# Low parts of three of a pair's five plain activation blocks made by GpSimd instead of VectorE, block means turned with two value tiles

## The chip, the cores and the metric

The kernel runs on one core of one Trainium2 chip. The metric is the device time of one launch in microseconds (us), less is better. Five engines with a queue each work side by side: TensorE (PE in the rows; its weight loads are PEld), VectorE (DVE), ScalarE (ACT), GpSimd (POOL), and SyncE (SP), which here only issues DMA transfers. Each queue is worked off in order; an instruction that has to wait holds up all that stand behind it on its engine.

## What is computed

The reference is a local attention with block summaries, followed by two feed-forward layers:

```
k_sum = k.reshape(B, H, nb, block, D).max(axis=3)
v_sum = v.reshape(B, H, nb, block, D).mean(axis=3)
scores_l = where(|i - j| < 16, scale * q k^T, -1e9)
scores_s = scale * q k_sum^T + log(block)
a = softmax(concat(scores_l, scores_s))
x = a @ concat(v, v_sum)                      # 2 batches, 8 heads, 768 tokens, 64 wide
xn = x / rms(x) * rms_g                       # 1536 tokens x 512
y  = (silu(xn @ w_gate) * (xn @ w_val)) @ w_out      # 512 -> 1536 -> 512
out = (s * relu(y @ w_in)**2 + b) @ w_out2           # 512 -> 2048 -> 512
```

A block is 32 tokens, so there are 24 block sums per head. The weights come in double precision.

## The kernel before

**Number format.** Every operand of a dense product is split into a high part (the value rounded to the format that TensorE takes at full pace) and a low part (value minus high part), and a product is three matmuls: high x high, low x high, high x low. For weights, ScalarE scales a loaded 128x512 unit (line 243), VectorE puts bits together in three instructions (lines 253 to 255), ScalarE makes the high part (line 268) and GpSimd the low part (line 272). One such unit is wanted every few microseconds for nearly the whole run, and a helper that is called at fixed places of the code (`slot`, `w_ahead`, `feed`) writes these steps between the others.

**Attention.** It runs in the first 110 us: 12 tiles of 128 tokens. A planner (`give_out`, line 472) sets the order: it holds a list of tasks, each with engine, assumed duration, rank and what it depends on, plays them on five assumed clocks, and writes the instructions of a task when its turn comes. The order inside each engine's queue is thus fixed when the program is built. Where the planner finds TensorE with nothing to do, it writes a filler matmul (line 557). For the first batch the value rows are turned on TensorE from a tile with the head dimension on partitions (`turn_v`, line 400): 12 windows of 96 rows, each put to its place by ScalarE or VectorE (`put_w`, lines 407 and 409). Under the 96 rows of each window stand 24 rows of block means. The first NMEAN windows get them from an additional set of four turning matmuls (line 398, which reads the 24 block sums that VectorE makes, line 387, as well), the others by a DMA that copies the 24 rows from windows 0 and 1 (`spread_v`; line 172 issues every transfer). The product of weights and values (line 740) of a tile waits for its windows and their means.

**First feed-forward layer.** Gate and value products (`gate`, `val`, `mm12`: lines 903, 904, 909) of a hidden unit are three groups of 12 matmuls, one for each 512 tokens. Between them stand "pairs" (`pair`, lines 1266 to 1268), in which two hidden units of 128 meet w_out in a scheme of seven products in place of eight for the first 1024 tokens; the last 512 tokens are done plainly. A pair needs nine activation blocks, each 128x512 with high and low part: five plain ones (b11, b21, b22, z0, z1: an activation as it is) and four combinations (t1 to t4, made by GpSimd at line 1116). `blocks` writes these out and `split` makes the two parts: the high part on ScalarE (line 1080 or 1082), the low part at line 1083 on the engine that it is given. Pairs 2, 4 and 6 go through `blocks` (pair 0 has its own function, and pair 2 has the b11 and z0 of its first unit ready from elsewhere, so that only z1, b21 and b22 of its plain blocks are split here).

**PSUM.** In this stage the products take turns on seven banks; an eighth is scratch for the weight bits. A bank comes free when VectorE has read it: line 1053 (gate: needs ScalarE's tanh of line 1052 first), line 1065 (value) or line 1274 (pair). When all seven are full, TensorE waits.

**Order of the stage.** gate 6, val 6, pair 2, gate 7, val 7, pair 4, gate 8, gate 9, pair 6, val 8, val 9. The blocks of pair 2 are made during gate and val 6, those of pair 4 during gate and val 7, those of pair 6 during gates 8 and 9. Low parts and combinations stand on the queues of VectorE and GpSimd between the weight work of the same time.

Of the kernel before, what the change touches and what calls it, by code (L numbers as in the profile page):

```python
# [38 lines left out]
PAIRS = (0, 2, 4, 6)  # L39
OUT = 4  # L40
TURN = (0,)
NMEAN = 4
LAT = 0.09
AHEAD = 4.0
IDLE = 0.6
# [13 lines left out]
def kernel(ctx: ExitStack, tc: tile.TileContext, q_t, k_t, v_w, v_t, w_gate, w_val, w_out, w_in2, w_out2, vecs, out):  # L59
    nc = tc.nc  # L60
# [31 lines left out]
    def r(ap):  # L92
        return ap.bitcast(F32R)
# [90 lines left out]
    def after(d, fn):  # L184
        later[d].append(fn)
# [15 lines left out]
    for kind, m in order:  # L201
# [6 lines left out]
        elif kind in ("gates", "vals"):  # L208
            n, ws = len(units), w_gate if kind == "gates" else w_val
            units += [ws[m], ws[m + 1], n, n + 1]  # L210
        elif kind == "pair":
            n = len(units)
            units += [w_out[m], w_out[m + 1], n, n + 1]
        elif kind == "two":
            n = len(units)
# [169 lines left out]
    def sum_vt(b, j):  # L385
        c0 = j * 128 + KW
        nc.vector.tensor_reduce(out=vs[:, c0:c0 + NS], in_=vt0[:, j * KL + WIN:j * KL + WIN + SEQ].rearrange("p (n i) -> p n i", i=BLK), axis=AX.X, op=ALU.add)

    def mean_vt(b, i):
        ps = mean_ps[b] = bank(i)  # L390
        for j in range(NPAIR):
            nc.tensor.transpose(ps[:, j * 128:(j + 1) * 128], vs[:, j * 128:(j + 1) * 128], ident)

    def turn_v(b, w, i, mean):
        ps = mean_ps[b, w] = bank(i)
        for j in range(NPAIR):
            if mean:
                nc.tensor.transpose(ps[0:KC, j * 128:(j + 1) * 128], vs[:, j * 128:j * 128 + KC], ident)
            k0 = j * KL + HQ * w
            nc.tensor.transpose(ps[0:KW, j * 128:(j + 1) * 128], vt0[:, k0:k0 + KW], ident)  # L400

    def put_w(b, w, eng, mean):
        rows = KC if mean else KW
        o = vslot(b, w)[0:rows, :, 0:HD]
        a = mean_ps[b, w][0:rows].rearrange("p (h d) -> p h d", d=HD)
        if eng == "DVE":
            nc.vector.tensor_scalar(out=o, in0=a, scalar1=share[0:rows], scalar2=None, op0=ALU.mult)
        else:
            nc.scalar.activation(out=o, in_=a, func=AF.Copy, scale=share[0:rows])

    def put_v(b, s, eng):
        o = vslot(b, s)[KW:KC, :, 0:HD]
        a = mean_ps[b][KW:KC].rearrange("p (h d) -> p h d", d=HD)
        if eng == "DVE":
            nc.vector.tensor_scalar(out=o, in0=a, scalar1=1.0 / BLK, scalar2=None, op0=ALU.mult)
        else:
            nc.scalar.activation(out=o, in_=a, func=AF.Copy, scale=1.0 / BLK)

    def spread_v(b, s0, n):
        a = vst[b][0][KW:KC, 0:2].rearrange("p (o e) h d -> p o (e h d)", o=1).broadcast_to([NS, n // 2, 2 * NH * VH])  # L420
        o = vst[b][s0 // NTL][KW:KC, s0 % NTL:s0 % NTL + n]
        fetch(out=o.rearrange("p (o e) h d -> p o (e h d)", e=2), in_=a)
# [40 lines left out]
    def task(eng, us, fn, deps=(), rank=0.0, take=(), give=(), bank=None, free=(), more=0.09):  # L463

        t = dict(eng=eng, us=us, fn=fn, deps=[d for d in deps if d is not None], rank=rank, take=take, give=give,
                 bank=bank, free=free, more=more, end=None)
        tasks.append(t)
        return t
# [91 lines left out]
    def dve(n):  # L560
        return 0.07 + 1.042e-3 * n

    def act(n):
        return 0.13 + 0.74e-3 * n

    def pl(n):
        return 0.1 + 2.42e-3 * n
# [4 lines left out]
    def plan(x):  # L572
# [15 lines left out]
        def lvt(b, j, rank):  # L588
            VL[b, j] = task("SP", mb(128 * KL * 4), lambda: load_vt(b, j), [SV[0, j], *(WT[0, w] for w in range(2 * NTL))] if b else (), rank=rank)
# [23 lines left out]
        def means(b, rank):  # L613
            if b == 0:
                zero.append(task("POOL", pl(512) / 3, lambda: nc.gpsimd.memset(vs, 0.0), rank=-28))
            sums = [task("DVE", dve(768), lambda j=j: sum_vt(b, j), [VL[b, j], *zero, *([VM[0]] if b else ())], rank + 0.1 * j) for j in range(NPAIR)]
            for j in range(NPAIR):
                SV[b, j] = sums[j]
            if b in TURN:
                puts = {}  # L620
                for w in range(2 * NTL):
                    m = w < NMEAN
                    rw = (rank + 1.5 + 0.4 * w) if w < 4 else w - 4.0 + 12 * b
                    T = WT[b, w] = task("PE", 0.88 if m else 0.44, lambda i, w=w, m=m: turn_v(b, w, i, m),
                                        [*([*sums] if m else [VL[b, j] for j in range(NPAIR)]), *([VM[0]] if b else ()), ci], rw, bank="M")
                    e = "ACT" if w % 4 != 1 else "DVE"
                    puts[w] = task(e, act(512) if e == "ACT" else dve(512), lambda w=w, e=e, m=m: put_w(b, w, e, m), [T, O[b, w // 2]], rw, free=(T,))
                    VM[b, w // 2, "ok"] = [puts[k] for k in range(w // 2 * 2, w + 1)]
                    if b == 1 or w == 2 * NTL - 1:
                        VM[b] = T  # L630
                if NMEAN < 2 * NTL:
                    for t, n in ((2, 2), (3, 6)):
                        spr = task("SP", 0.3 * n, lambda t=t, n=n: spread_v(b, 2 * t, n), [puts[0], puts[1], O[b, 0], *[O[b, k] for k in range(t, t + n // 2)]], 2 * (6 * b + t) - 6)
                        for k in range(t, t + n // 2):
                            VM[b, k, "ok"].append(spr)
            else:
                tr = VM[b] = task("PE", 0.44, lambda i: mean_vt(b, i), [*sums, ci], rank + 1.5, bank="M")
                puts = []
                for s in range(4 if b == 0 else 2):
                    e = ("ACT", "DVE")[s % 2]  # L640
                    puts.append(task(e, act(512) if e == "ACT" else dve(512), lambda s=s, e=e: put_v(b, s, e), [tr, O[b, s // 2]], rank + 1.5 + s // 2))
                for p in puts[:-1]:
                    puts[-1]["deps"].append(p)
                puts[-1]["free"] = (tr,)
                for t in range(NTL):
                    if b == 0 and t < 2 or t == 0:
                        VM[b, t, "ok"] = puts[2 * t:2 * t + 2]
                    else:
                        if t in (1, 2 if b == 0 else 1, 3):
                            n = 6 if t == 3 else 2 if b == 0 else 4  # L650
                            spr = task("SP", 0.3 * n, lambda t=t, n=n: spread_v(b, 2 * t, n), [*puts[0:2], *[O[b, k] for k in range(t, t + n // 2)]], 2 * (6 * b + t) - 6)
                        VM[b, t, "ok"] = [spr]
            if b == 0:
                for j in range(NPAIR):
                    lvt(1, j, 5.5 + j)
# [36 lines left out]
        for n, (i, g) in enumerate(us):  # L692
            b, t = divmod(i, NTL)
# [137 lines left out]
        for s in range(NSUB):  # L831
            for j in range(HEAD):
# [43 lines left out]
                d = task("ACT", act(512), lambda f=do_v: f(1), [c, *((*free_of[j], box.get("hi")) if s == 0 else ())], rr)  # L876
# [68 lines left out]
    def moe(x, ps_a, ps_b):  # L945
# [128 lines left out]
        def units_of(t, n):  # L1074
            a = t[:, 0:2 * n * SUB].rearrange("p (k e c) -> p k e c", k=n, e=2)
            return [a[:, k] for k in range(n)]

        def split(d, a, eng, n):
            if n == 0:
                nc.scalar.activation(out=r(d[:, 0]), in_=a, func=AF.Copy)  # L1080
            else:
                after(n - 1, lambda: nc.scalar.activation(out=r(d[:, 0]), in_=a, func=AF.Copy))
            after(n, lambda: eng.tensor_tensor(out=r(d[:, 1]), in0=a, in1=d[:, 0], op=ALU.subtract))
# [44 lines left out]
        def blocks(p, j, s, u):  # L1128
            if p not in D:
                d = D[p] = D[4] if 4 in D else dict(zip(("b11", "b21", "b22", "t1", "t2", "t3", "t4", "z0", "z1"),  # L1130
                                                        units_of(big(1), 3) + units_of(big(4), 3) + units_of(big(0), 3)))
            d = D[p]
            B[j, s] = u
            if s == 2:
                split(d[f"z{j}"], u, nc.vector, 0)
            elif s == 0:
                split(d["b21" if j else "b11"], u, nc.vector, 0)
            elif j == 0:
                split(d["t1"], minus(0, u, B[0, 0]), nc.gpsimd, 1)
            else:  # L1140
                split(d["b22"], u, nc.vector, 0)
                split(d["t2"], minus(1, u, B["t"][:, 0]), nc.gpsimd, 1)
                split(d["t3"], minus(2, u, B[0, 1]), nc.gpsimd, 1)
                split(d["t4"], minus(3, B[1, 0], B["t"][:, 1]), nc.gpsimd, 1)
# [341 lines left out]
    n = 2 * HEAD + MORE  # L1486
# [86 lines left out]
```

## Time and profile before

| | us |
|---|---|
| three runs | 621.99, 622.53, 624.09 |
| median | 622.53 |
| the profiled execution | 625.98 |
| its span, first to last instruction | 624.2 |

The profiled execution is 1.78 us longer than its span, and 3.45 us longer than the median of the runs. Rows of a timeline give the start (us from the start of the span), the duration, engine, source line, operation, output and inputs by the program's names, and the number of instructions merged; a bracket at the end gives the idle time of the engine just before and what ended it. A matmul's duration overlaps with the next one's: how fast TensorE goes is read from the distance of starts.

### The profile page before, as it was taken

The numbers are of one execution on the slowest core, as the hardware profiler recorded it, in microseconds if no ns is written. First come the engines' busy times: TensorE is split into PE (matmuls) and PEld (weight loads), VectorE is DVE, ScalarE is ACT, GpSimd is POOL, SyncE is SP. The second block draws the span as 40 slices with busy tenths as digits, with TensorE's granted clock in tenths as the row PEclk, the third lists the DMA queues.
The fourth block names the chain that finished last, engine by engine and source line by source line (L and its number), as shares of the span: only waits on it lengthen the run. The fifth ranks groups of instructions, "written<-read, shape, count | busy, mean of one in ns | idle before, by whom it ended". The sixth has DMA issues, their size and how long they took to land.

```text
span 624.2 us, 10061 instructions
## 1 busy us (share of the span) xinstructions
PE 606.1 (97%) x3754; PEld 498.2 (80%) x3754; DVE 481.3 (77%) x862; ACT 312.9 (50%) x619; POOL 335.3 (54%) x371
## 2 busy tenths in 40 slices
PE   5998999999999999989999999999999999999998
PEld 3877778888888887868888888888888888888886
DVE  5698898969795899999786768792679767876732
ACT  2897975635357252442343336754672267326700
POOL 2266855559366868575573667453545544554400
PEclk9999999999999999999999999999999999999999
DMA  8997320012222223231432100043003400310022
GB/s 282 279 310 242 107 70 2 0 35 101 65 71 87 85 70 132 69 120 49 130 107 69 34 1 0 2 150 121 2 0 106 164 1 0 106 64 1 1 102 101
DMA packets 17017, 53.56 MB, mean 86 GB/s; under 512 B 1904, under 2 KB 2160, under 8 KB 16968
## 3 DMA queue, kind: packets, MB, share of 16 engines
q1 hardware_dynamic: 16968, 52.92, 25.9%
q8 instruction: 29, 0.48, 0.3%
q14 instruction: 20, 0.16, 0.1%
HBM read 48.86 MB, written 3.15 MB: 83 GB/s over the span
## 4 chain that ended last, share of the span: by engine, by line
PE 85%; DVE 10%; issue 2%; DMA 2%; ACT 1%; DVEq 0%
PE b L909 9%; PE b L903 9%; PE b L904 9%; PE b L1440 7%; PE b L1437 7%; PE b L1438 7%; PE b L1365 5%; PE b L1341 4%; PE b L1339 4%; PE b L1340 4%; PE b L1367 2%; PE b L740 2%; DVE part L1274 2%; PE b L684 2%; PE b L1266 2%
## 5 line engine op out<-in xcount | busy, mean ns | idle before, releaser
L272 POOL TENSOR_TENSOR wl<-wa,wh 128x512 fp32r<-128x512 f32 x68 | 89.8, 1322 | 67.4 <-ACT wh L268 65.5
L903 PE MATMUL b<-x,wh 128*128 128x512 f32 x240 | 94.8, 395 | 0.0
L904 PE MATMUL b<-x,wl 128*128 128x512 f32 x240 | 93.5, 390 | 0.0
L243 ACT ACTIVATE wa<-raw 128x512 f32<-128x512 f32 x68 | 45.0, 667 | 68.1 <-DMA raw<-in_w_out_dram 30.2
L1438 PE MATMUL b<-wl,hg 128*128 128x512 f32 (+1 forms) x196 | 75.1, 385 | 0.0
L1437 PE MATMUL b<-wh,hg 128*128 128x512 f32 (+1 forms) x196 | 75.1, 385 | 0.0
L268 ACT ACTIVATE wh<-wa 128x512 fp32r<-128x512 f32 x68 | 42.8, 630 | 57.6 <-PE b L1268 25.2
L272 POOL TENSOR_TENSOR wl<-ws,wh 128x512 fp32r<-128x512 f32 x28 | 37.3, 1342 | 52.0 <-ACT wh L268 50.3
L909 PE MATMUL b<-x,wh 128*128 128x512 f32 x240 | 65.2, 393 | 0.0
L1350 DVE SCALAR_TENSOR_TENSOR b<-b,vec,u 128x512 f32<-128x512 f32 x48 | 35.9, 758 | 35.6 <-ACT u L1349 35.4
L1440 PE MATMUL b<-wh,hg 128*128 128x512 f32 (+1 forms) x196 | 58.0, 385 | 0.0
L903 PEld LDWEIGHTS b<-x,wh 128*128 128x128 f32 x240 | 45.1, 188 | 9.3
L904 PEld LDWEIGHTS b<-x,wl 128*128 128x128 f32 x240 | 45.1, 188 | 8.9
L909 PEld LDWEIGHTS b<-x,wh 128*128 128x128 f32 x240 | 44.4, 188 | 9.1
L281 POOL TENSOR_TENSOR ws<-wa 128x128 f32<-128x128 f32 x56 | 33.3, 595 | 32.5 <-DVE wa L255 32.4
L1349 ACT ACTIVATE u<-b 128x512 f32<-128x512 f32 x48 | 28.3, 597 | 37.7 <-DVE b L1374 27.5
L1446 DVE TENSOR_TENSOR part<-b,part 128x512 f32<-128x512 f32 (+1 forms) x37 | 24.3, 671 | 25.1 <-PE b L1440 25.1
L752 POOL TENSOR_TENSOR sm<-sm,mone 128x4 f32<-128x4 f32 x24 | 26.2, 1099 | 32.4 <-ACT sm L749 31.5
L1437 PEld LDWEIGHTS b<-wh,hg 128*128 128x128 f32 x196 | 36.8, 188 | 7.4
L1438 PEld LDWEIGHTS b<-wl,hg 128*128 128x128 f32 x196 | 36.8, 188 | 7.4
L1440 PEld LDWEIGHTS b<-wh,hg 128*128 128x128 f32 x196 | 36.4, 188 | 7.3
L1365 PE MATMUL b<-y,wh 128*128 128x512 f32 x128 | 41.8, 389 | 0.0
(214 smaller groups left out, 1553.9 us busy)
## 6 DMA issues: line engine op xcount, KB each, us to landing
raw<-in_w_out_dram SPq DMA_DIRECT2D x28, 512.0 KB, 3.6
raw<-in_w_in_dram SPq DMA_DIRECT2D x16, 512.0 KB, 3.6
raw<-in_w_gate_dram SPq DMA_DIRECT2D x12, 512.0 KB, 3.6
raw<-in_w_val_dram SPq DMA_DIRECT2D x12, 512.0 KB, 4.0
hg<-in_k_t_dram SPq DMA_DIRECT2D x8, 400.0 KB, 5.3
vt<-in_v_t_dram SPq DMA_DIRECT2D x8, 400.0 KB, 4.4
part<-in_v_w_dram SPq DMA_DIRECT2D x6, 528.0 KB, 5.9
q<-in_q_t_dram SPq DMA_DIRECT2D x12, 256.0 KB, 5.3
```

The costliest lines, as they stand in the source:

```text
L243: nc.scalar.activation(out=a, in_=raw_t[i][:, :, 1].bitcast(F32), func=AF.Copy, scale=2.0 ** -112)
L268: nc.scalar.activation(out=r(h), in_=a_t[i], func=AF.Copy)
L272: nc.gpsimd.tensor_tensor(out=r(lo), in0=a_t.pop(i), in1=high[i], op=ALU.subtract)
L281: nc.gpsimd.tensor_tensor(out=o, in0=x0, in1=x1, op=op)
L903: nc.tensor.matmul(ps, r(hi[:, kk * 128:(kk + 1) * 128]), xh, start=kk == 0, stop=False)
L904: nc.tensor.matmul(ps, r(lo[:, kk * 128:(kk + 1) * 128]), xh, start=False, stop=False)
L909: nc.tensor.matmul(ps, r(hi[:, kk * 128:(kk + 1) * 128]), r(act(kk, 1)), start=False, stop=kk == 3)
L1350: after(0, lambda: nc.vector.scalar_tensor_tensor(out=a, in0=a, scalar=sbc[:, 0:1], in1=u, op0=ALU.mult, op1=ALU.mult))
L1365: nc.tensor.matmul(bank, r(aw[k][0][:, cs]), r(d), start=e + k + j == 0, stop=e + k + j == 3)
L1437: nc.tensor.matmul(acc, gh, r(ws[e][0][:, cs]), start=start and n == 0, stop=False)
L1438: nc.tensor.matmul(acc, gh, r(ws[e][1][:, cs]), start=False, stop=False)
L1440: nc.tensor.matmul(acc, r(ge[n][:, 1]), r(ws[e][0][:, cs]), start=False, stop=stop and n == len(es) - 1)
```

## The change

Two things are changed. (1) In `blocks`, `split` of z0, z1 and b22 gets GpSimd in place of VectorE for the low part: 8 instructions of line 1083 (z1 and b22 for pair 2; z0, z1 and b22 for pairs 4 and 6). b11 and b21 stay on VectorE. (2) NMEAN goes from 4 to 2: only windows 0 and 1 get their block means on TensorE; windows 2 and 3 get them by one more `spread_v` DMA. The planner is not changed, but it plays the shorter list, and so the order of the attention stage comes out otherwise on all engines.

```
-NMEAN = 4
+NMEAN = 2
...
                 if NMEAN < 2 * NTL:
-                    for t, n in ((2, 2), (3, 6)):
+                    for t, n in ((1, 2), (2, 2), (3, 6)):
                         spr = task("SP", 0.3 * n, lambda t=t, n=n: spread_v(b, 2 * t, n), ...
...
             if s == 2:
-                split(d[f"z{j}"], u, nc.vector, 0)
+                split(d[f"z{j}"], u, nc.gpsimd, 0)
...
             else:
-                split(d["b22"], u, nc.vector, 0)
+                split(d["b22"], u, nc.gpsimd, 0)
```

VectorE's queue during gate 8, the blocks of pair 6, before. Names: `hg` holds the blocks, `t` and `u` are activations, `wa` and `raw` weight units, `b_` a PSUM bank; line 1083 is a low part, line 1053 empties a bank of a gate product:

```order
L253 TENSOR_SCALAR b_3206<-wa 128x512
L254 SCALAR_TENSOR_TENSOR b_3206<-raw,b_3206 128x512
L255 SCALAR_TENSOR_TENSOR wa<-raw,b_3206 128x512
L1083 TENSOR_TENSOR hg<-t,hg 128x512
L1083 TENSOR_TENSOR hg<-u,hg 128x512
L1053 SCALAR_TENSOR_TENSOR u<-u,b_3150 128x512
```

and now:

```order
L253 TENSOR_SCALAR b_3199<-wa 128x512
L254 SCALAR_TENSOR_TENSOR b_3199<-raw,b_3199 128x512
L255 SCALAR_TENSOR_TENSOR wa<-raw,b_3199 128x512
L1053 SCALAR_TENSOR_TENSOR u<-u,b_3143 128x512
```

The two low parts (z0, z1) in front of the bank's release are gone. The same holds at gate 7 for pair 4.

GpSimd's queue during gate and val 7, the blocks of pair 4, as a difference (`wl` is a weight's low part, `ws` sums of weights; line 1116 makes a combination, line 1083 with `hg<-hg` the low part of one):

```order
 L272 TENSOR_TENSOR wl<-wa,wh 128x512
-L272 TENSOR_TENSOR wl<-ws,wh 128x512 x2
+L272 TENSOR_TENSOR wl<-ws,wh 128x512
+L1083 TENSOR_TENSOR hg<-u,hg 128x512 x2
+L272 TENSOR_TENSOR wl<-ws,wh 128x512
 L1116 TENSOR_TENSOR hg<-u 128x512
 L272 TENSOR_TENSOR wl<-wa,wh 128x512
```

z0 and z1 now stand ahead of a weight's low part and of all the combinations; b22 (not in this piece) stands ahead of the low parts of t2, t3 and t4.

SyncE's queue in the attention stage, where the copied means (`hg<-hg`) stand among the loads of keys, queries, weights (`raw`) and the second batch's values (`vt`), as a difference:

```order
 L172 DMA hg<-in_k_t_dram 128x800 x2
-L172 DMA hg<-hg 24x1056
+L172 DMA hg<-hg 24x1056 x2
 L172 DMA hg<-hg 24x3x1056
 L172 DMA hg<-in_k_t_dram 128x800 x2
+L172 DMA q<-in_q_t_dram 128x512
 L172 DMA raw<-in_w_gate_dram 128x1024
-L172 DMA q<-in_q_t_dram 128x512
-L172 DMA raw<-in_w_val_dram 128x1024
 L172 DMA q<-in_q_t_dram 128x512
 L172 DMA vt<-in_v_t_dram 128x800 x2
```

One copy is added ahead of two key loads, a query goes ahead of a weight, and a weight goes behind value loads.

## Rows read from the trace of the kernel before

**Rows 1.** The page's part 1: engine, busy us, share of span, instructions.

```profile
PE 606.1 (97%) x3754; PEld 498.2 (80%) x3754; DVE 481.3 (77%) x862; ACT 312.9 (50%) x619; POOL 335.3 (54%) x371
```

**Rows 2.** Busy time by stretch: length, then us and instructions of each engine, clock, DMA.

```profile
14.00:56.00 42.00, 38.12 (x713) 32.22 (x713) 34.35 (x132) 36.59 (x102) 18.96 (x28) 1.00 0.89 291
...
213.80:279.90 66.10, 62.67 (x273) 50.60 (x272) 64.24 (x90) 27.52 (x49) 47.11 (x46) 1.00 0.27 88
...
300.00:600.00 300.00, 300.00 (x1326) 248.39 (x1325) 220.30 (x315) 145.07 (x248) 153.82 (x154) 1.00 0.17 56
```

**Rows 3.** Waits of TensorE, 238 to 289 us: us in total, times, longest.

```profile
PE b L1266 <- DVE u L1053: 2.1, 2, 1.1
PE b L1266 <- DVE u L1065: 1.3, 2, 1.1
```

**Rows 4.** Timeline of TensorE: starts of pair 2, pair 4, gate 8, pair 6, val 8.

```profile
206.86 0.39 PE L1266 MATMUL b<-hg,wh 128*128 128x512 f32 x1
...
238.14 0.39 PE L1266 MATMUL b<-hg,wh 128*128 128x512 f32 x1
...
254.97 0.39 PE L903 MATMUL b<-x,wh 128*128 128x512 f32 x1
...
271.29 0.39 PE L1266 MATMUL b<-hg,wh 128*128 128x512 f32 x1
...
288.99 0.39 PE L903 MATMUL b<-x,wh 128*128 128x512 f32 x1
```

**Rows 5.** Timeline of VectorE around the low parts of pairs 4 and 6.

```profile
227.07 3.18 DVE L1083 TENSOR_TENSOR hg<-u,hg 128x512 fp32r<-128x512 f32 x2
...
240.57 1.36 DVE L1083 TENSOR_TENSOR hg<-u,hg 128x512 fp32r<-128x512 f32 x1
241.86 0.67 DVE L1065 SCALAR_TENSOR_TENSOR u<-u,b 128x512 f32<-128x512 f32 x1
...
260.98 1.50 DVE L1083 TENSOR_TENSOR hg<-t,hg 128x512 fp32r<-128x512 f32 x1
262.41 1.78 DVE L1083 TENSOR_TENSOR hg<-u,hg 128x512 fp32r<-128x512 f32 x1
...
266.83 0.69 DVE L1083 TENSOR_TENSOR hg<-t,hg 128x512 fp32r<-128x512 f32 x1
...
274.59 1.37 DVE L1083 TENSOR_TENSOR hg<-u,hg 128x512 fp32r<-128x512 f32 x1
275.89 0.67 DVE L1053 SCALAR_TENSOR_TENSOR u<-u,b 128x512 f32<-128x512 f32 x1
```

**Rows 6.** GpSimd: line 1083 from 190 to 290 us (busy us, mean ns), then timeline.

```profile
L1083 POOL TENSOR_TENSOR hg<-hg 128x512 fp32r<-128x512 f32 x12 | 16.1, 1375 | 0.0
...
205.14 1.29 POOL L272 TENSOR_TENSOR wl<-wa,wh 128x512 fp32r<-128x512 f32 x1
...
238.81 5.52 POOL L1083 TENSOR_TENSOR hg<-hg 128x512 fp32r<-128x512 f32 x4
...
261.89 1.75 POOL L1116 TENSOR_TENSOR hg<-t 128x512 f32<-128x512 f32 x1
267.36 1.32 POOL L272 TENSOR_TENSOR wl<-wa,wh 128x512 fp32r<-128x512 f32 x1 [3.71 <-ACT wh L268]
...
272.85 5.50 POOL L1083 TENSOR_TENSOR hg<-hg 128x512 fp32r<-128x512 f32 x4
```

**Rows 7.** Timeline of ScalarE: the last two tanh of gate 9.

```profile
273.47 1.08 ACT L1052 ACTIVATE u<-b 128x512 f32<-128x512 f32 x2
```

**Rows 8.** Timeline of TensorE in the attention stage: turning windows, and a wait.

```profile
18.07 0.27 PE L398 MATMUL b<-ident,vt 128*120 128x128 f32 x1
18.18 0.27 PE L400 MATMUL b<-ident,vt 128*96 128x128 f32 x1
...
49.25 0.62 PE L740 MATMUL b<-hg,PT 120*64 120x66 f32 x13 [1.35 <-issue]
```

**Rows 9.** Timeline of SyncE's queue: the two copies of the means.

```profile
20.35 2.11 SPq L172 DMA_DIRECT2D hg<-hg  x2
```

## The prediction

> **What bounds the kernel now.** I read the page's busy shares first, then busy time by stretch, then TensorE's waits, then the timelines of the engine that was waited for. TensorE is busy for 97% of the span [rows 1], and from 300 to 600 us without a gap [rows 2], so a change can only pay where TensorE stands still, or by taking matmuls away. Gaps of size are in two places that the change touches: 42.00 - 38.12 = 3.9 us between 14 and 56 us, in the attention, and 66.10 - 62.67 = 3.4 us between 213.8 and 279.9 us [rows 2]. In the second VectorE is busy for 64.24 of 66.10 us, GpSimd for 47.11 [rows 2]. All four waits of TensorE there are for VectorE to empty a bank: two for line 1065, two for line 1053 [rows 3].
>
> What these waits cost in all is more than their idle time. From gate 8 to pair 6 TensorE starts 72 matmuls in 271.29 - 254.97 = 16.32 us, 0.2267 us each, undisturbed [rows 4]. From the start of pair 4 to that of val 8 it starts 66 + 72 + 66 = 204 matmuls; at that pace they take 46.2 us, and they took 288.99 - 238.14 = 50.85 [rows 4]. So 4.6 us are lost, 1.9 in pair 4 (254.97 - 238.14 = 16.83 for 66, which want 14.96) and 2.7 in pair 6.
>
> Why VectorE is late there: line 1083. Two low parts take 3.18 us ahead of gate 7's banks; a third takes 1.36 us right ahead of the line 1065 that TensorE waits for [rows 5]. For pair 6 two take 3.28 us and one 1.37 us, the last right ahead of the line 1053 at 275.89 that ends a wait [rows 5].
>
> **The change part by part.** *The moved low parts.* Off VectorE's queue go 8 instructions, 2 for pair 2 and 3 each for pairs 4 and 6. By the rows those of pair 4 hold its queue for 3.18 + 1.36 = 4.5 us and those of pair 6 for 1.50 + 1.78 + 1.37 = 4.65 us [rows 5]; neighbours overlap by some 0.08 us, so 4.4 us each. Pair 4: the line 1065 at 241.86 comes 4.4 us earlier, against 1.9 us lost, so TensorE doesn't wait; VectorE has then no backlog when gate 8 begins. Pair 6: by its own three alone the release at 275.89 + 0.67 = 276.6 comes at 272.2, and TensorE, which had waited for it for 1.1 us [rows 3] and is 1.9 us earlier by then, wants that bank at 276.6 - 1.1 - 1.9 = 273.6. That is a margin of 1.4 us, without what VectorE wins by beginning gate 8 on time. So I take the whole 4.6 us as gained; the lower end is 3.5 (a rest of 1.1 in pair 6, the first rival). More than 4.6 is excluded here, since TensorE's own pace is the bound then.
>
> *The same work on GpSimd.* Its twelve line-1083 instructions take 1.375 us on average [rows 6], so it has 3 x 1.375 = 4.1 us more to do for pairs 4 and 6 each, and 2.75 for pair 2. In the stretch it is idle for 66.10 - 47.11 = 19 us [rows 2], 11 of which these take up. Is a low part late? Pair 4: z0 and z1 are made with gate 7, well ahead of 238.14. The low parts of t1 to t4 run from 238.81 for 5.52 us [rows 6]; with z0 and z1 ahead of them t1 is done at 238.81 + 1.38 + 2.75 = 242.9, and with b22 behind t1 the others at 245.7, 247.0 and 248.4. Pair 4 uses t1 after 39 matmuls, at 238.14 + 39 x 0.2267 = 247.0, t2 at 247.7, t3 at 248.3, t4 at 251.7. So all are in time, t3 by the least, 1.3 us. Pair 6 is alike: 272.85 + 5.50 + 4.1 = 282.5 for the last by the old clock, but GpSimd had idled for 3.71 us at 267.36 for ScalarE's high part of a weight [rows 6], and line 268 reads what VectorE's line 255 writes; with VectorE 4 us earlier that idle time takes in the added work. Pair 2 has the least room: GpSimd's low part at 205.14 + 1.29 = 206.4 belongs to weights that pair 2, from 206.86, uses after 18 matmuls, at 210.9 [rows 4, 6]. With 2.75 us more it is done at 209.2, 1.7 us early. So the cost of this is nothing as long as GpSimd's queue is not over 1.7 us later than I count; what it costs when it is, is the second rival.
>
> *Means by copying.* Eight matmuls of line 398 go. They start 0.11 us apart [rows 8], so 0.9 us of TensorE's queue goes, ahead of tile 1's scores. Added is one copy of 24 rows: two took 2.11 us of SyncE's queue [rows 9], so about 1.06 us, with key loads, queries, weights and the second batch's values queued behind it. Nobody needs those at once: the DMA engines are busy for 0.89 of the stretch [rows 2], but none of TensorE's gaps of over half a microsecond that I read was ended by one of these loads for certain; the longest, 1.35 us at 49.25, is put to nothing the profile shows [rows 8]. The new wait is tile 1's values product for the copy issued at 20.35; between nothing and the copy's own 1.06 us, I take nothing, since tile 1's scores, exponentials and turning all come after tile 0's. What I can't work out is the re-planned order from 20 to 80 us. ScalarE and VectorE are at 36.59 and 34.35 of 42.00 us there [rows 2], so part of the 0.9 us is hidden behind them; I take 0.6 us as gained. For its bounds I let the new order give back or add half of the idle 3.9 us, 1.9 either way: from 2.5 gained to 1.3 lost.
>
> *Sum.* 4.6 + 0.6 = 5.2 us. Against the profiled execution: 625.98 - 5.2 = 620.8. The median of the runs stands 3.45 us below that execution, and the loss is counted in matmuls that each run makes, so the same goes off it: 622.53 - 5.2 = 617.3.
>
> **The rivals.** *A rest of the wait stays.* Line 1053 of gate 9 needs ScalarE's tanh, and the last two ran from 273.47 to 274.55 [rows 7], behind high parts of t2 to t4 that wait for GpSimd. If that clock stays, the bank's release can't come before 274.1 + 0.67 = 274.7, while TensorE wants it at 273.6, as above: 1.1 us stay, 618.4.
>
> *GpSimd becomes the late one.* The row shows that a two-input instruction on the other engine can stretch one: the same low part took 0.69 us at 266.83 with GpSimd idle, and 1.78 us at 262.41 beside GpSimd's instruction of 1.75 us [rows 5, 6]. The Trainium skill says the same as a rule (SBUF — State Buffer, "Who interferes with whom"): a VectorE instruction with two SBUF inputs and a GpSimd instruction that reads SBUF exclude each other for the whole instruction, and who comes first blocks the other. Moved instructions now meet b11 and b21 that way; by the rule alone the sum would stand at this rival's. By rows: of line 1083 and 1116 a pair has now ten instructions on GpSimd. If each takes 1.75 us in place of 1.375, the last is 3.75 us later than I count, 2.4 over the room of 1.3 in pairs 4 and 6 and, with eight, 1.3 over that of pair 2: 6 us. With two thirds of it, 617.3 + 4 = 621.3. Against it speak GpSimd's 19 idle us.
>
> *The new order of the attention is worse.* In the changed program the first dense matmuls (line 903) stand on TensorE's queue behind one more tile of scores and two more value products than before. If TensorE waits there for exponentials as long as it waits in all that stretch now, 3.9 us are added: 622.53 - 4.6 + 3.9 - 0.6 = 621.2.
>
> *ScalarE passes GpSimd's lateness on: slower.* ScalarE's queue has the high parts of t2 to t4 ahead of tanh. If GpSimd's combinations come there later by three stretched instructions, 3 x 1.75 = 5.25 us, the second tanh ends at 274.55 + 5.25 = 279.8 and its bank is free at 280.5, 3.9 us after the 276.6 of now: the old waits stay, and one grows: 622.53 - 0.6 + 3.9 = 625.8. It decides once the combinations of pair 6 end 1 us later than the 272.85 of now [rows 6].
>
> *It does nothing*: the banks are held up by something that moves along. Then only the turning is left, 621.9. Rows 5 speak against it: the low part stands right ahead of the release, twice.
>
> **How the numbers follow.** Forecast 0.62; rest of the wait 0.13; GpSimd late 0.08; order worse 0.09; ScalarE 0.04; nothing 0.04. A measurement of this kernel tells 0.3% from no change, 1.9 us: faster is below 620.7, slower above 624.4. The first two cases, with the attention's bounds, lie between 615.4 and 619.7; with the spread of the runs (0.5 us below the median) the low end is 614.8. To leave out no more than 2 in 10, the high end goes to 621.4, which takes in most of the order's case. Faster: 0.62 + 0.13 and some 0.05 of the two middle cases, 0.80; same: 0.14; slower: 0.06.
>
> **What would show it.** Between the starts of pair 4 and val 8 some 46.3 us instead of 50.85, and no wait of line 1266 for VectorE; VectorE's share between 214 and 280 down by some 9 us, GpSimd's up by 11; pair 2's start at most 1 us earlier than 206.86 and TensorE's idle time up to 56 us about as before. It would be wrong if lines 1266 to 1268 wait for GpSimd or ScalarE, or if pair 2 begins later than 206.86.

## The result and the profile after

| | before | changed |
|---|---|---|
| four runs each, us | 621.99, 622.53, 624.09, 624.29 | 617.31, 617.63, 618.93, 619.22 |
| median | 623.31 | 618.28 |
| ratio of changed to before | | 0.991, interval 0.988 to 0.993 |
| the profiled execution, its span | 625.98, 624.2 | 617.31, 615.5 |

The change is faster, by 5.0 us between the medians. The two profiled executions lie 8.7 us apart; the 3.7 us between these figures are followed up below. One execution in all the sets below, 760.25 us at a granted clock of 0.758 in the run with three transfers, is slow and left out of that run's figures. First the page's part 1 and, from part 4, the chain of work that ended last, by engine (of the kernel before, TensorE had 85% of it and VectorE 10%):

```profile
PE 603.3 (98%) x3746; PEld 497.6 (81%) x3746; DVE 471.6 (77%) x854; ACT 312.9 (51%) x619; POOL 341.8 (56%) x379
...
PE 94%; ACT 3%; DMA 1%; DVE 0%; issue 0%; POOL 0%; ACTq 0%
```

All waits of TensorE in the changed kernel (us in total, times, longest). None is for VectorE's lines 1053 and 1065, in answer to [rows 3]; those that are left all lie in the attention stage:

```profile
PE b L684 <- DMA q<-in_q_t_dram: 4.6, 1, 4.6
PE b L740 <- ACT PT L731: 1.7, 5, 0.5
PE b L684 <- DMA hg<-in_k_t_dram: 1.3, 1, 1.3
PE b L684 <- DVE km L377: 0.8, 3, 0.4
PE b L789 <- DVE xn L781: 0.4, 1, 0.4
```

The starts on TensorE that answer [rows 4]: pair 2, pair 4, gate 8, pair 6, val 8:

```profile
202.72 0.39 PE L1266 MATMUL b<-hg,wh 128*128 128x512 f32 x1
...
234.00 0.39 PE L1266 MATMUL b<-hg,wh 128*128 128x512 f32 x1
...
248.96 0.39 PE L903 MATMUL b<-x,wh 128*128 128x512 f32 x1
...
265.28 0.39 PE L1266 MATMUL b<-hg,wh 128*128 128x512 f32 x1
...
280.24 0.39 PE L903 MATMUL b<-x,wh 128*128 128x512 f32 x1
```

From pair 4 to val 8 it is 46.24 us in place of 50.85: 4.61 us gained, and 204 matmuls at 0.2267 us each, TensorE's own pace. From pair 2 to pair 4 it is 31.28 us in both. Pair 2 itself starts 4.14 us earlier than in [rows 4]. Busy time by stretch (length; then PE, PEld, DVE, ACT, POOL; clock; DMA), first for the stretches that answer [rows 2], the second moved by 4.14 us:

```profile
14.00:56.00 42.00, 39.99 (x791) 33.63 (x791) 36.87 (x144) 38.45 (x106) 22.00 (x29) 1.00 0.90 294
209.66:275.76 66.10, 66.10 (x294) 54.72 (x293) 64.23 (x96) 27.62 (x49) 54.48 (x53) 1.00 0.30 96
300.00:600.00 300.00, 300.00 (x1325) 248.43 (x1324) 214.78 (x306) 142.38 (x243) 149.38 (x151) 1.00 0.18 55
```

TensorE fills the second stretch wholly, 294 matmuls in place of 273. VectorE is as busy in it as before, with six instructions more; so the fair comparison is by the same work, from the start of gate 7 to that of val 8, of before and then of the changed kernel:

```profile
221.82:288.99 67.17, 63.74 (x277) 51.49 (x276) 65.37 (x94) 27.53 (x50) 45.68 (x42) 1.00 0.29 94
```

```profile
217.68:280.24 62.56, 62.56 (x277) 51.80 (x276) 60.69 (x89) 27.63 (x50) 51.12 (x48) 1.00 0.32 101
```

For this work VectorE needs 4.7 us less and GpSimd 5.4 us more. The timeline of VectorE, where [rows 5] had the low parts in front of the releases:

```profile
225.66 2.98 DVE L1083 TENSOR_TENSOR hg<-u,hg 128x512 fp32r<-128x512 f32 x2
...
234.01 0.68 DVE L1065 SCALAR_TENSOR_TENSOR u<-u,b 128x512 f32<-128x512 f32 x1
...
256.94 1.76 DVE L1083 TENSOR_TENSOR hg<-t,hg 128x512 fp32r<-128x512 f32 x1
258.62 1.78 DVE L1083 TENSOR_TENSOR hg<-u,hg 128x512 fp32r<-128x512 f32 x1
...
265.77 0.68 DVE L1053 SCALAR_TENSOR_TENSOR u<-u,b 128x512 f32<-128x512 f32 x1
```

Only b11 and b21 are left there, and they run beside GpSimd's instructions: two take 2.98 us, the others 1.76 and 1.78, where one took 0.69 with GpSimd idle [rows 5]. GpSimd, where [rows 6] had it: the group of all low parts of combinations from 190 to 290 us, then its timeline:

```profile
L1083 POOL TENSOR_TENSOR hg<-hg 128x512 fp32r<-128x512 f32 x12 | 15.3, 1294 | 0.0
```

```profile
225.09 3.00 POOL L1083 TENSOR_TENSOR hg<-u,hg 128x512 fp32r<-128x512 f32 x2
...
238.55 3.80 POOL L1083 TENSOR_TENSOR hg<-hg 128x512 fp32r<-128x512 f32 x3
...
268.21 3.77 POOL L1083 TENSOR_TENSOR hg<-hg 128x512 fp32r<-128x512 f32 x3
```

GpSimd's last low part for pair 4 is done at 242.3, 8.3 us after pair 4's start; pair 4 uses t4, the last one, 13.5 us after its start by the prediction's count. In pair 6 it is 6.7 us.

### The profile page after: what moved, and what is told of

Read it like the earlier page. It is cut to its first block, busy times and chain, and to the rows that moved or that the text cites. A ratio compares the mean times of both kernels' runs of the same rounds, so it can differ in the third digit from the quotient of the medians.

```text
span 615.5 us, 10058 instructions
## 1 busy us (share of the span) xinstructions
PE 603.3 (98%) x3746; PEld 497.6 (81%) x3746; DVE 471.6 (77%) x854; ACT 312.9 (51%) x619; POOL 341.8 (56%) x379
## 4 chain that ended last, share of the span: by engine, by line
PE 94%; ACT 3%; DMA 1%; DVE 0%; issue 0%; POOL 0%; ACTq 0%
PE b L903 11%; PE b L909 11%; PE b L904 11%; PE b L1437 7%; PE b L1440 7%; PE b L1438 7%; PE b L1365 5%; PE b L1341 4%; PE b L1339 4%; PE b L1340 4%; PE b L1266 3%; PE b L1267 3%; PE b L1268 3%; PE b L1367 2%; PE b L740 2%; ACT P L710 1%
```

## The experiments

Theory: the 4.6 us come from the low parts alone, by way of VectorE's queue, and the rest of the gain from the attention. Rival: most of the gain comes from the attention, whose end (pair 2's start) moved by 4.1 us in the profile.

**The two halves.** The low parts alone:

```
-                split(d[f"z{j}"], u, nc.vector, 0)
+                split(d[f"z{j}"], u, nc.gpsimd, 0)
...
-                split(d["b22"], u, nc.vector, 0)
+                split(d["b22"], u, nc.gpsimd, 0)
```

> Only the low parts of z0, z1 and b22 move to GpSimd; the block means stay as before. My theory (the dense stage loses 4.6 us in pairs 4 and 6 to VectorE's queue, and the low parts alone are the cause): from pair 4's start to val 8's 46.2 us in place of 50.85, no wait of line 1266 for VectorE, and pair 2 begins where it begins before (206.9, within 0.5); time 4.6 us below the kernel before, ratio 0.9926. Rival (most of the gain comes from the attention's new order, since pair 2 begins 4.1 us earlier in the profile of the changed kernel): the ratio is 0.995 or nearer to 1.

Measured: 619.68 us, ratio 0.9935, interval 0.991 to 0.996. From pair 4 to val 8 46.24 us, no wait of line 1266; pair 2 at 207.34. The block means alone:

```
-NMEAN = 4
+NMEAN = 2
...
-                    for t, n in ((2, 2), (3, 6)):
+                    for t, n in ((1, 2), (2, 2), (3, 6)):
```

> Only the block means change (two windows turned with their means, the rest copied); all low parts stay as before. My theory by the sum on record: 0.6 us less, ratio 0.999, pair 2's start 0.6 us earlier, the dense stage with the waits of before (50.9 us from pair 4 to val 8). Rival, by the start of pair 2 in the two profiles (206.86 and 202.72): 4 us less, ratio 0.9935. A third: the 4 us between the profiles are mostly the execution, not the program; then the ratio stands between, at 0.997 to 0.999, and the stalls put to no releaser (0.80 at 29.45, 1.35 at 49.25) come and go between executions of one program.

Measured: 623.61 us, ratio 0.9993, interval 0.997 to 1.0015. From pair 4 to val 8 50.83 us, with the waits of [rows 3] to the digit (TensorE's waits from 200 to 300 us):

```profile
PE b L1266 <- DVE u L1053: 2.1, 2, 1.1
PE b L1266 <- DVE u L1065: 1.3, 2, 1.1
```

So the dense gain belongs to the low parts alone. Pair 2 starts at 206.91, as before, though every queue holds the changed kernel's order up to the blocks of pair 2. Each of the two kernels was run again:

> The kernel before against itself: how far two sets of executions of one program lie apart, and whether its attention stage looks alike in another profile. If the order sets it, pair 2 begins at 206.9 within 0.5 again and the stalls of 0.80 us at 29.45 and 1.35 us at 49.25, which the profile puts to no releaser, are there again. If the execution sets it, pair 2 begins up to 3 us earlier and one or both are gone. Ratio 1.000 within 0.002 by either.

Measured: ratio 0.9998, interval 0.997 to 1.002. Pair 2 at 205.90, the stall of 0.80 us now 0.63, that of 1.35 gone: the execution sets a good part of it. The dense stage differs too: from pair 4 to val 8 it is 49.75 us, a loss of 3.5 us and not 4.6, since only one of the two waits for line 1053 is there.

> The changed kernel again, on the same chip as the two halves. Ratio 0.991 within 0.002. If the two halves add, this ratio less 1 is the sum of theirs. By the order pair 2 begins at 202.7 within 0.5 again; by the execution it moves by a microsecond or more.

Measured: 618.17 us, ratio 0.9903, interval 0.988 to 0.993. Pair 2 at 203.71. Together the two halves bring 0.0097 and by themselves 0.0065 and 0.0007; each interval is some 0.0023 to either side, so whether they add to the last 0.0025 (1.6 us) isn't told.

**Which low parts.** Only z0 and z1 (the first pair of lines above), then only b22 (the second):

> Only the low parts of z0 and z1 move to GpSimd (five instructions); b22 stays on VectorE, and the block means stay as before. My theory, by the busy time taken off VectorE's queue against what each pair had lost (1.9 us in pair 4, 2.7 in pair 6): 3.2 us less for pair 4 and 3.2 for pair 6, so both losses go; from pair 4 to val 8 46.2 to 46.5 us, ratio 0.993. Rival (all three have to move, since b22 stands right ahead of the release that TensorE waits for): one wait for VectorE stays in each pair, 48 us or more.

Measured: ratio 0.9936, interval 0.991 to 0.996; 46.53 us from pair 4 to val 8, and no wait. As the theory had it.

> Only the low part of b22 moves to GpSimd (three instructions). My theory by the same count: 1.36 of 1.9 us go in pair 4 and 1.37 of 2.7 in pair 6, so from pair 4 to val 8 48.1 us in place of 50.85, and waits of line 1266 for VectorE of some 2 us stay; ratio 0.9955. Rival (what stands right ahead of the release is what counts): 46.5 us or less.

Measured: ratio 0.9932, interval 0.990 to 0.996; 47.20 us, one wait left (of 200 to 300 us):

```profile
PE b L1266 <- DVE u L1065: 0.3, 1, 0.3
```

Pair 4 keeps a loss of 252.07 - 236.50 - 14.96 = 0.61 us (0.5 expected), pair 6 one of 0.35 (1.3 expected). So the count by busy time holds for pair 4, the first to lose; in pair 6 more goes than its own low part, since VectorE no longer begins gate 8 late. Neither end is right by itself: z alone does nearly all, b22 alone four fifths, and the two overlap.

**How much more GpSimd can take.** All five:

```
-                split(d["b21" if j else "b11"], u, nc.vector, 0)
+                split(d["b21" if j else "b11"], u, nc.gpsimd, 0)
```

> The changed kernel with b11 and b21 on GpSimd as well: all five plain low parts, 1.3 us each more. My theory (GpSimd has room: in the profile of the changed kernel its last low part for pair 4 is done 3 us before its use, and VectorE is no longer waited for): no change against the changed kernel, 46.2 us from pair 4 to val 8, ratio 0.991 to the kernel before. Rival (GpSimd becomes the late one, by the room of 1.3 us that the prediction counted): 2.6 - 1.3 = 1.3 us lost in each of the two pairs, 48.8 us, ratio 0.995.

Measured: 618.65 us, ratio 0.989, interval 0.985 to 0.993; 46.24 us from pair 4 to val 8. VectorE's busy time from gate 7 to val 8 falls to 55.2 us, and nothing is gained by it, since TensorE was the bound already. GpSimd is at 54.7 of 62.6 us and still not late for pairs 4 and 6; pair 2, which has one more low part on GpSimd as well, takes 15.35 us in place of 14.96. Then four and two instructions more in front of a pair's combinations (here four):

```
-                split(d["t1"], minus(0, u, B[0, 0]), nc.gpsimd, 1)
+                split(d["t1"], [minus(0, u, B[0, 0]) for _ in range(5)][-1], nc.gpsimd, 1)
```

> The changed kernel with four more GpSimd instructions of 128x512 ahead of the first combination of pair 4 and of pair 6 (each makes that combination again, so the work is only repeated), 4 x 1.26 = 5.0 us later on its queue. If GpSimd's room is what the profile of the changed kernel shows (t3's low part done 3.1 us ahead of its use in pair 4, 4.6 in pair 6): 1.9 and 0.4 us lost, 48.5 us from pair 4 to val 8, and the waits are for GpSimd in lines 1266 to 1268. If the room is the 1.3 us counted in the prediction: 3.7 lost in each, 53.6 us. If ScalarE passes the lateness on through tanh: line 1266 to 1268 or 903 wait for VectorE again, on lines 1053 and 1065.

Measured: 622.49 us, ratio 0.996, interval 0.994 to 0.999; 50.36 us. TensorE's waits are not for GpSimd but for VectorE again:

```profile
244.97 0.50 PE L1266 MATMUL b<-hg,wh 128*128 128x512 f32 x1 [1.57 <-DVE u L1065]
...
278.51 0.50 PE L1266 MATMUL b<-hg,wh 128*128 128x512 f32 x1 [1.73 <-DVE u L1053]
```

The waits of ScalarE and of VectorE from 230 to 290 us, then ScalarE's timeline, show how the lateness got there. ScalarE's high parts (line 1082) wait for GpSimd's combinations, and other steps stand behind them on its queue. In pair 4 it is the scaling of a weight (line 243), for which VectorE's line 253 waits 3.6 us with line 1065 behind it; in pair 6 it is tanh (line 1052), for which VectorE's release waits:

```profile
ACT hg L1082 <- POOL hg L1116: 15.8, 8, 7.7
```

```profile
DVE b L253 <- ACT wa L243: 3.6, 1, 3.6
DVE u L1053 <- ACT u L1052: 3.2, 2, 1.7
```

```profile
276.62 0.63 ACT L1082 ACTIVATE hg<-hg 128x512 fp32r<-128x512 f32 x1 [0.62 <-POOL hg L1116]
277.16 1.07 ACT L1052 ACTIVATE u<-b 128x512 f32<-128x512 f32 x2
```

> As the run with four repeated GpSimd instructions, with two: 2 x 1.26 = 2.5 us later on GpSimd's queue in pairs 4 and 6. With four (5.0 us) pair 4 lost 17.05 - 14.96 = 2.1 us and pair 6 2.0, through ScalarE's tanh and VectorE's release of the bank. If that is a room that is used up and then one for one, the room is 5.0 - 2.1 = 2.9 us in each, and 2.5 us cost nothing: 46.2 us from pair 4 to val 8. If lateness costs from the start in proportion, 1 us is lost in each: 48.3 us. If the room is the 1.3 us that the prediction counted for GpSimd: 1.2 us in each, 48.6 us.

Measured: 618.99 us, ratio 0.992, interval 0.989 to 0.995; 46.24 us. So 2.5 us more cost nothing and 5.0 us cost 2.1 us in pair 4 and 2.0 in pair 6: a room that lies between, 2.9 us if it is used up one for one.

**What moves pair 2's start.** The profiles of all runs with four transfers, sorted by the order of the attention stage. "Second block" is the time at which a packet of the DMA queue named instruction (the one that serves TensorE, as is shown below) is recorded, read in quarters of a us; stalls are TensorE's idle times "<-issue" from 14 to 60 us, for which the profile shows no releaser:

| profile | first turning | second block | stalls | pair 2 | pair 4 to val 8 |
|---|---|---|---|---|---|
| before | 14.27 | 27.00 | 0.80, 1.35 | 206.86 | 50.85 |
| before again | 14.15 | 27.00 | 0.63 | 205.90 | 49.75 |
| low parts only | 14.59 | 28.50 | 2.87 | 207.34 | 46.24 |
| z0, z1 only | 14.04 | 25.25 | none | 204.01 | 46.53 |
| b22 only | 14.62 | 26.50 | none | 205.22 | 47.20 |
| changed | 13.84 | 24.75 | none | 202.72 | 46.24 |
| changed again | 14.86 | 24.50 | 0.75 | 203.71 | 46.24 |
| means only | 14.56 | 27.25 | 0.91, 1.22 | 206.91 | 50.83 |
| all five | 14.26 | 24.50 | none | 203.53 | 46.24 |
| two more on GpSimd | 14.16 | 26.25 | 0.80 | 204.39 | 46.24 |
| four more on GpSimd | 14.49 | 23.75 | none (2.15 put to VectorE) | 206.53 | 50.36 |

The first five have the old order, the others the new one. Within an order pair 2's start spreads over 3.3 and 4.2 us, and it goes largely with the stalls. The stall at 28 to 31 us stands in front of the same matmul in every profile of the old order that has it; here of the low parts only, then of before:

```profile
27.92 0.25 PE L684 MATMUL b<-km,q 64*64 64x24 f32 x6
31.04 0.18 PE L684 MATMUL b<-km,q 64*64 64x24 f32 x1 [2.87 <-issue]
```

```profile
28.40 0.25 PE L684 MATMUL b<-km,q 64*64 64x24 f32 x6
29.45 0.18 PE L684 MATMUL b<-km,q 64*64 64x24 f32 x1 [0.80 <-issue]
```

Each of the eight stalls "<-issue" in the table ends 2.0 to 2.8 us after the record of such a packet of 16 KB. Busy time from the start of the span to just ahead of the two stalls of before, with the number of matmuls and then of weight loads in parentheses, shows what the packets hold:

```profile
0.00:29.44 29.44, 21.37 (x348) 17.11 (x349) 18.13 (x54) 15.34 (x36) 8.21 (x35) 1.00 0.87 275
...
0.00:49.24 49.24, 38.58 (x727) 31.20 (x727) 36.74 (x129) 33.28 (x88) 19.44 (x52) 1.00 0.89 293
```

Counted like this, all eight stalls stand behind 348 or 349, 601, or 727 or 728 matmuls, in either order. These places lie 126 to 127 matmuls apart or twice that; with the weight loads that is some 253 instructions, and a profile has 29 of these packets for some 3750 matmuls and as many weight loads, 259 to a packet. So the packets are blocks of TensorE's instructions, and in each stall TensorE had run out of them. The question left is what makes a block late; the loads are one candidate, with the DMA engines busy for 0.89 of this stage [rows 2]. Line 40 sets how many of SyncE's transfers may be under way, and leaves every order as it is:

```
-OUT = 4
+OUT = 8
```

> The changed kernel with eight of SyncE's transfers under way at a time in place of four (line 40); every queue holds the same instructions in the same order. It tests what TensorE's stalls without a releaser in the attention stage are. In nine profiles a stall, where there is one, ends 2.2 to 3.2 us after a block of the DMA queue named instruction has landed, and where the second block lands by 26 us there is none, where it lands at 27.0 to 28.5 there is one of 0.6 to 2.9 us. If blocks of instructions are held up by the loads in flight: with a deeper queue the second block lands at 28 us or later, there are stalls of 3 us or more in total between 14 and 60 us, and pair 2 begins at 205.5 or later (202.7 to 203.7 in undisturbed profiles of the changed kernel); ratio to the kernel before 0.993 or more. If the loads don't matter: blocks and pair 2's start as in the changed kernel, ratio 0.990.

Measured: 624.27 us, ratio 1.001, interval 0.999 to 1.002, with the dense stage undisturbed (46.24 us). Pair 2 at 209.69. TensorE's waits without a releaser are four, with 5.84 us:

```profile
PE b L684 <- issue: 4.0, 3, 2.5
PE b L740 <- issue: 1.8, 1, 1.8
```

The blocks in front of them are recorded at 26.0, 33.5, 41.75 and 50.0 us, and the stalls end at 28.43, 36.23, 44.14 and 52.53: again 2.0 to 2.8 us behind, and behind 349, 475, 601 and 728 matmuls. All nine executions have a mean granted clock of 0.995 or 0.997, where all ten of the changed kernel have 0.999 or 1.000. The second block came 1.3 us later than in the changed kernel and not the 3 us expected; what grew most are the later stalls. With three transfers:

> The changed kernel with three transfers under way in place of four, the same order on every queue. If blocks of instructions are held up by the loads in flight: the second block lands before 25 us, no stall without a releaser, and the times lie closer together; whether the median falls below the changed kernel's 618.2 depends on what the thinner stream costs (waits for DMA in lines 684 and 740): by the stalls seen in the changed kernel (0, 0, 0.75 and one of 2.15 us) at most 1 us less, ratio 0.989. If the loads don't matter: stalls as often as before, ratio 0.990 to 0.992.

Measured: no stall without a releaser, the second block at 23.5 us, but ratio 1.000, interval 0.998 to 1.002: 6 us more than the changed kernel. A part goes with the clock: eight of the eleven executions have a mean granted clock of 0.995 to 0.997 and a median of 625.0 us, the three at 1.00 take 621.55 to 623.12, so that 3 to 5 us remain for the thinner stream of loads. In the profile, one of these three, pair 2 starts at 207.12, and the waits of the attention are for other engines and the data behind them (longest 1.9 us, for ScalarE's line 731). My bound of 1 us less was wrong about what that costs, and so was the expectation that the times would lie closer together: they spread over 5 us. So four under way is better than three and eight. That loads in flight delay the blocks is supported by the 5.84 us of stalls with eight, twice the most that any profile with four has, but not shown: the second block's 26.0 us lies within what four gave in this order (23.75 to 27.25), there is one profile each with three and with eight, and four also gives profiles without a stall, so that the one with three tells little.

## Why the prediction was right

**The dense stage** was right: no wait for VectorE, and 46.24 us where some 46.3 were forecast. The step that carried it was to count matmuls at TensorE's own pace (0.2267 us) in place of adding up idle times: the four waits of [rows 3] add up to 3.4 us, the loss was 4.6. One step in it was too simple: "the loss is counted in matmuls that each run makes". The pace is the same in each execution, the loss is not: three profiles with the old low parts lose 4.6, 4.6 and 3.5 us. By the times, the low parts alone gained a ratio of 0.0065, 4.1 us (2.6 to 5.5).

**The median.** 617.3 was forecast, 618.28 measured, 0.98 above and inside the range. The difference was forecast as 5.2 us and is 5.0 beside the runs of the same time. The base was low: 622.53 came from three runs, and 83 runs of the kernel before, all taken with the experiments and the result, have a median of 624.2, against 618.2 for ten of the changed kernel: 6.0 us. With that base the forecast's sum gives 619.0; the base was 1.7 us low and the gain 0.8, and that these offset each other in part is luck.

**The attention's term** stays open within its bounds. I had 0.6 us, between 1.3 lost and 2.5 gained. The run of the means alone, the only direct test, gave 0.4 us (0.9 lost to 1.9 gained), not told from nothing. By the table without its last row, whose clock fell, pair 2's start less the first turning and less the stalls is 190.4 us on average in the five profiles of the old order (189.9 to 191.1) and 189.2 in the five of the new one (188.1 to 190.2): 1.2 us gained, within my bounds and twice my value; the two ranges overlap, and it is assumed that a stall costs its length. What I read as one execution's idle time [rows 2, 8] was in large part its stalls, which the next execution hasn't or has elsewhere. So the forecast "pair 2 at most 1 us earlier" failed: it came 4.14 us earlier, of which 2.15 were stalls and 0.43 the first loads. "TensorE's idle time up to 56 us about as before" failed for the same reason (2.0 us between 14 and 56, against 3.9).

**The copy** was priced at 1.06 us of SyncE's queue. It took twice that, 2.1 us more than the two of [rows 9]; the three together:

```profile
19.03 4.20 SPq L172 DMA_DIRECT2D hg<-hg  x3
```

It cost nothing visible: no wait of line 740 for a copy stands among TensorE's waits above.

**Busy shares.** I forecast VectorE's share down by 9 us and GpSimd's up by 11 between 214 and 280; for the same work it is 4.7 and 5.4 us. Two steps failed. For VectorE I took off the six low parts of pairs 4 and 6, 4.4 us each pair, and left the others as they were. Its line 1083 fell by 7.5 us there (14.1 to 6.6), since the four low parts that stay went from some 5.0 to 6.6 us in all beside GpSimd; of the rest a part is one more instruction of line 1274 in the stretch. For GpSimd I counted all eight, while two belong to pair 2's blocks, made earlier. The six take 8.2 us, and GpSimd's other instructions there became shorter: the low parts of the combinations went from 1.42 to 1.29 us each, four of the combinations from 1.53 to 1.30.

**The rivals.** *A rest of the wait stays* fell: the last two tanh start at 266.30 us in the changed kernel, 7.2 us earlier than in [rows 7] (4.1 of it by the start of pair 2), since what they wait for on GpSimd comes earlier too. *GpSimd becomes the late one* fell: seven of the eight moved instructions take some 1.3 us and one 1.75, and GpSimd's room is at least 2.5 us and not the 1.3 that I counted. I had started from old times, in which VectorE's low parts stretched GpSimd's instructions (t1 to t4's low parts took 5.52 us in pair 4 [rows 6], now 1.31 and 3.80) and GpSimd waited for ScalarE's weights (3.71 us in pair 6 [rows 6]). The Trainium skill's rule (SBUF — State Buffer, "Who interferes with whom") is borne out by what it does to VectorE: 2.98 us for two instructions at 225.66 beside GpSimd's 3.00 for two at 225.09, against 0.69 for one alone [rows 5]. It didn't decide, for what is stretched was no longer on the path. *ScalarE passes GpSimd's lateness on* has the right engine and the wrong threshold: ScalarE does pass it on, in pair 6 through tanh and in pair 4 through line 243, once GpSimd is 5.0 us later than in the changed kernel, and not at 2.5. *The new order is worse* and *it does nothing* fell with the two halves.

## What to carry to other kernels

Count what a stage loses as its matmuls at an undisturbed pace, not as the sum of its idle times; the time that is left came out to the hundredth here, while the loss itself differed between executions. Before idle time in a stage full of loads is given to a change, look at the same stage in a second execution: stalls that the profile puts to no releaser may belong to the execution and not to the order. Work moved to an engine that waits can cost less than its length (here 5.4 us for 8.2), and its lateness reaches the bound engine by the queue of a third one, so look there for the limit.

## What the runs showed of the hardware

**TensorE can run out of instructions.** Its short matmuls use them up fast: in the attention stage of before, 713 matmuls and as many weight loads are recorded in 42 us [rows 2], and blocks came every 5 to 9 us (27.00, 32.75, 38.75, 47.00, 53.25). Where one came late, TensorE stood still for 0.6 to 2.9 us. In the dense stage, at some 4.4 matmuls per us, no such stall is seen. The Trainium skill (Runtime: NRT & Kernel Launch, "Instruction fetch mechanics") has the blocks, 16 KiB each, fetched ahead by a DMA queue of their own, and calls the cost of a block's edge mostly hidden; the size agrees with the 16 KB packets here, the cost does not hold here, in a stage where the DMA engines are busy for 0.9 of the time [rows 2]. That the packets are TensorE's is shown by the count: the 13 stalls stand behind 348 or 349, 475, 601, 727 or 728, and 854 matmuls and nowhere else. What delays a block is not shown.

**A stall can take the clock along.** In the run with four more GpSimd instructions TensorE stood still for 2.15 us up to 56.63. The profile names VectorE's line 703; but the stall stands behind 854 matmuls, one block further than the 728 of others, and the packet that goes with it is recorded at 53.5, some 3 us before its end. So it is most likely one more of these stalls. The granted clock behind it stands third from the end of the row in these two stretches:

```profile
54.00:58.00 4.00, 1.85 (x6) 1.19 (x5) 3.26 (x20) 1.81 (x5) 3.83 (x7) 0.83 0.82 274
58.00:62.00 4.00, 4.00 (x17) 3.18 (x16) 0.99 (x4) 1.66 (x5) 0.12 (x2) 0.74 0.68 199
```

These are means over time at 2.4 and at 1.2 GHz: behind the stall, matmuls of line 903 and 904 start 0.42 to 0.43 us apart in place of 0.23. In the run with eight transfers the stall of 1.85 us that ended at 52.53 was followed by 0.66 between 54 and 58 us; the stall of 2.87 us in the profile of the low parts alone was not followed by a lower clock. Which stalls bring it is left open. What such an execution costs, the stall included, can be read from whole executions: of 79 of the kernel before whose clock is listed, 16 have a mean clock of 0.996 or 0.997 and a median of 626.8 us, the other 63 one of 623.6. None of the ten of the changed kernel is of that kind, so the difference of the medians depends in part on how many of each were drawn.
